# Attention with tiles 0 and 1 of the scores in the same banks, 1e-9 added by GpSimd, and a new order of all operations

## The chip, the cores and the metric

The kernel runs on one core of a Trainium2 chip. The metric is the device time of one execution in microseconds (us). The kernel before has a median of 1025.54 us over three runs (1025.2 to 1026.46).

## The reference

Three stages follow one another: a forgetting attention, a mixture layer with softplus and a second one with a gate. Cut to what is computed:

```python
# q, k, v: (4, 8, 576, 64), f: (4, 8, 576)
scores = q @ k.T / sqrt(64) + (cum[:, None] - cum[None, :])   # cum = cumsum(log(clip(f, 1e-4, 1)))
scores = where(causal, -1e9, scores); scores -= max(scores)
attn = exp(scores); attn = attn / (sum(attn) + 1e-9)
x = attn @ v                                  # -> (2304 tokens, 512)
x = softplus(x @ w_in) @ w_out                # d_ff = 2048
out = (sigmoid(x @ w_gate) * (x @ w_val)) @ w2_out   # d_ff = 1536
```

## The kernel before

All products are made in split precision: a matrix is a high part, rounded for TensorE (names with h), and a low part that is the rest (names with l), and a product is three matmuls of these parts (four for scores, with one that adds the decay rows `nb`).

The attention goes over 16 pairs p, each two heads of one batch entry. One pair is a list of operations, methods of `Attention` with the pair and a tile number:

- `load_q`, `load_k`, `load_v`, `decay_rows` are loads issued by SyncE (SP). `qh`, `kh`, `ql`, `kl`, `v_high`, `v_low` split them on GpSimd (POOL).
- `scores(i)`: row blocks of 128 queries of the two heads. Causality lets row block i of head 0 and block 8 − i of head 1 go as one step (tiles i and 8 − i); their widths are in `W9`, 128 to 512. Each is four pairs of matmuls over half the rows of the array, into two PSUM banks of the tag `s` (lines 223). The last block, tile 4, takes eight matmuls of 288 columns into the tile X (line 212).
- `minimum(t)`, VectorE (DVE), line 230: adds the causal mask, scales by −1/8 and takes the row minimum, so it reads `s`. `exp(t)`, ScalarE (ACT), line 235: exponential and row sum.
- `transposes(g)`, TensorE (PE), line 254: seven groups of up to four 128 x 128 blocks of the exponentials into a bank of the tag `t`, which has two banks. `evac_h(g)` on ScalarE (line 276) and `evac_l(g)` on VectorE (line 280) take the high and low part out.
- `rinv`: sums + 1e-9 (line 286) and reciprocal (line 287), both on VectorE. `rinv_t`: TensorE transposes the reciprocals (line 292) into a bank of the tag `t`; `rinv_b`: ScalarE copies them (line 297); `rinv_c`, `rinv_d`: through DRAM they come back spread over all rows.
- `pv(h, j)`, line 330: transposed exponentials times v for head h, into the accumulators, tile Y for head 0 and tile X for head 1. X holds tile 4 of the scores as well, at another time. X and Y have two banks each.
- `out_a(h)` on ScalarE (line 340) copies half of an accumulator, `out_b(h)` on VectorE (line 345) adds the other half to it, `out_c` on GpSimd (line 348) multiplies by the reciprocals, `out_d` stores.

The order of all instructions is written out: `WHEN` gives each operation a number, pair p adds 9 p (`PERIOD`), and `Attention.run` sorts all of them and issues them in that order; every engine keeps the order of its own part. `START` replaces numbers for pair 0 and `END` for pair 15. Each engine then works its list strictly from the front, and waits for semaphores where data or a buffer isn't ready.

Into the same order go the steps that prepare the weights of the next stage (`Weights.op`): LOAD (512 KB by SP, line 480), SCALE and HI on ScalarE (lines 488, 493), SHIFT, LOW, SIGN on VectorE (lines 502, 504, 506), LO on GpSimd (line 496). `STEPS` and `LATE_STEPS` say when which step is due; a step that can't be done (its predecessor isn't there, or `limit` is reached) is skipped. `X_STEPS` does the same for loading the next stage's tokens (cast at line 551), `PRODUCTS` and `UNITS` for its first products. Behind the attention `Moe1` and the second layer run from their own loops; they are not touched.

Of the kernel before, what the change touches and what calls it, by code (L numbers as in the profile page):

```python
# [21 lines left out]
class Attention:  # L22
# [327 lines left out]
    def out_d(self, R, p):  # L350
# [14 lines left out]
        ("kl",): -9.0904, ("decay_rows",): -8.1126, ("scores", 4): -2.7503, ("scores", 3): -2.135,
        ("minimum", 4): -2.019, ("minimum", 3): -0.0192, ("minimum", 5): 0.3552, ("scores", 1): 2.0404,
        ("exp", 3): 2.9766, ("exp", 5): 3.066, ("minimum", 1): 3.0798, ("minimum", 7): 3.2918, ("scores", 0): 4.02,
        ("minimum", 0): 4.7488, ("minimum", 8): 4.7664, ("exp", 7): 4.9241, ("scores", 2): 5.5069,
        ("minimum", 6): 5.8865, ("exp", 0): 6.2356, ("minimum", 2): 6.379, ("exp", 1): 6.6423, ("exp", 4): 6.7033,
        ("exp", 2): 7.105, ("transposes", 0): 7.5695, ("load_v",): 7.7728, ("exp", 6): 7.8053,  # L370
        ("transposes", 1): 7.9929, ("exp", 8): 8.7191, ("evac_h", 0): 9.5166, ("evac_h", 1): 9.5706,
        ("rinv",): 10.083, ("v_high",): 10.1126, ("evac_l", 0): 10.4436, ("v_low",): 10.514,
        ("evac_l", 1): 11.2219, ("transposes", 2): 12.2269, ("evac_h", 2): 12.276, ("transposes", 3): 12.3519,
        ("evac_h", 3): 12.4099, ("evac_l", 2): 13.0431, ("rinv_t",): 13.1193, ("rinv_b",): 13.2113,
        ("evac_l", 3): 13.7368, ("transposes", 5): 13.8096, ("transposes", 4): 13.9726, ("evac_h", 5): 14.8574,
        ("pv", 0, 0): 14.9016, ("evac_h", 4): 14.9515, ("evac_l", 5): 15.137, ("pv", 0, 2): 15.291,
        ("evac_l", 4): 15.6663, ("transposes", 6): 15.699, ("evac_h", 6): 16.5991, ("evac_l", 6): 16.839,
# [785 lines left out]
```

## Time and profile before

| what | value |
|---|---|
| median of the runs | 1025.54 us |
| time of the profiled execution | 1027.21 us |
| its span | 1025.3 us |
| mean granted TensorE clock | 0.996 |
| TensorE busy | 1003.1 us, 98% of the span |
| VectorE busy | 609.5 us, 59% |
| ScalarE busy | 510.4 us, 50% |
| GpSimd busy | 147.2 us, 14% |
| attention | about 0 to 217 us |

The busy shares are means over stages. In the attention VectorE, ScalarE and GpSimd are busy for most of the time too; behind it GpSimd has next to nothing to do. The rows that count are in the section before the prediction.

### The profile page before, as it was taken

The numbers are of one execution on the slowest core, as the hardware profiler recorded it, in microseconds if no ns is written. First come the engines' busy times: TensorE is split into PE (matmuls) and PEld (weight loads), VectorE is DVE, ScalarE is ACT, GpSimd is POOL, SyncE is SP. The second block draws the span as 40 slices with busy tenths as digits, with TensorE's granted clock in tenths as the row PEclk, the third lists the DMA queues.
The fourth block names the chain that finished last, engine by engine and source line by source line (L and its number), as shares of the span: only waits on it lengthen the run. The fifth ranks groups of instructions, "written<-read, shape, count | busy, mean of one in ns | idle before, by whom it ended". The sixth has DMA issues, their size and how long they took to land.

```text
span 1025.3 us, 15871 instructions
## 1 busy us (share of the span) xinstructions
PE 1003.1 (98%) x5584; PEld 880.1 (86%) x5584; DVE 609.5 (59%) x1226; ACT 510.4 (50%) x1085; POOL 147.2 (14%) x154
## 2 busy tenths in 40 slices
PE   5999999999999999999999999999999999999998
PEld 4788877887788889988888889999999999999997
DVE  5999999877955666645636654445344343443333
ACT  4889988866644455445334544333334233333332
POOL 7667776610000000000000000000000000000000
PEclk8999999999999999999999999999999999999999
DMA  5355554534535656627525776865677666676631
GB/s 149 113 144 148 158 144 132 173 118 171 208 141 187 231 187 243 251 83 263 195 102 180 257 251 230 294 226 187 222 259 255 216 213 223 211 246 214 222 139 62
DMA packets 114698, 196.07 MB, mean 191 GB/s; under 512 B 14702, under 2 KB 38398, under 8 KB 114620
## 3 DMA queue, kind: packets, MB, share of 16 engines
q1 hardware_dynamic: 112684, 189.98, 55.3%
q10 hardware_dynamic: 1936, 5.09, 1.6%
q8 instruction: 44, 0.72, 0.3%
q14 instruction: 34, 0.28, 0.1%
HBM read 149.19 MB, written 45.83 MB: 190 GB/s over the span
## 4 chain that ended last, share of the span: by engine, by line
PE 87%; DMA 4%; DVE 4%; ACT 3%; issue 1%; SPq 1%; POOL 0%; ACTq 0%; DVEq 0%; POOLq 0%
PE z L559 9%; PE z L561 9%; PE z L560 9%; PE h L559 5%; PE h L560 5%; PE h L561 5%; PE x L330 5%; PE s L223 5%; PE t L254 4%; DMA raw_wi<-in_moe_w_in_dram 3%; PE oY L559 2%; PE oY L560 2%; PE oY L561 2%; PE oX L559 2%; PE oX L560 2%; PE oX L561 2%
## 5 line engine op out<-in xcount | busy, mean ns | idle before, releaser
L559 PE MATMUL z<-three,three 128*128 128x384 f32 x456 | 152.9, 335 | 0.1
L561 PE MATMUL z<-three,three 128*128 128x384 f32 x456 | 152.8, 335 | 0.0
L560 PE MATMUL z<-three,three 128*128 128x384 f32 x456 | 152.6, 335 | 0.0
L608 DVE TENSOR_TENSOR gl<-L,gh 128x512 fp32r<-128x512 f32 (+1 forms) x80 | 51.0, 637 | 109.1 <-ACT gh L607 105.4
L596 ACT ACTIVATE L<-h 128x512 f32<-128x512 f32 (+1 forms) x80 | 44.2, 553 | 140.0 <-PE h L561 140.0
L235 ACT ACTIVATE P<-P,m 128x128 f32<-128x128 f32 (+3 forms) x144 | 83.2, 581 | 9.2 <-DVE m L230 9.2
L559 PEld LDWEIGHTS z<-three,three 128*128 128x128 f32 x456 | 85.6, 188 | 1.8 <-DVE raw L869 0.5
L560 PEld LDWEIGHTS z<-three,three 128*128 128x128 f32 x456 | 85.6, 188 | 1.4
L561 PEld LDWEIGHTS z<-three,three 128*128 128x128 f32 x456 | 85.6, 188 | 0.0
L230 DVE CUSTOM_DVE_ANT_0 P<-s,mask 128x256 f32<-128x256 f32 (+3 forms) x144 | 70.6, 516 | 12.2 <-PE s L223 7.4
L559 PE MATMUL h<-xh,wi_h 128*128 128x512 f32 (+1 forms) x200 | 73.7, 368 | 0.0
L561 PE MATMUL h<-xh,wi_h 128*128 128x512 f32 (+1 forms) x200 | 73.6, 368 | 0.0
L560 PE MATMUL h<-xl,wi_h 128*128 128x512 f32 (+1 forms) x200 | 73.6, 368 | 0.0
L280 DVE TENSOR_TENSOR PTl<-t,PTh 128x512 fp32r<-128x512 f32 (+2 forms) x112 | 66.9, 619 | 5.0 <-ACT PTh L276 4.9
L856 ACT COPY bl<-z 128x384 f32<-128x384 f32 x36 | 17.3, 479 | 101.6 <-PE z L561 101.6
L868 DVE TENSOR_TENSOR raw<-z,bh 128x384 f32<-128x384 f32 x36 | 20.1, 557 | 76.3 <-PE z L561 76.3
L861 DVE TENSOR_TENSOR raw<-z,p 128x384 f32<-128x384 f32 x18 | 10.0, 558 | 93.1 <-PE z L561 79.2
L276 ACT CAST PTh<-t 128x512 fp32r<-128x512 f32 (+2 forms) x112 | 55.9, 536 | 18.1 <-PE t L254 17.7
L254 PE MATMUL t<-ident,P 128*128 128x128 f32 x400 | 60.2, 286 | 4.6 <-DVE PTl L280 3.2
L254 PEld LDWEIGHTS t<-ident,P 128*128 128x128 f32 x400 | 44.9, 143 | 17.3 <-issue 4.7
L890 ACT CAST gh<-raw 128x384 fp32r<-128x384 f32 x72 | 33.6, 514 | 48.6 <-DVE raw L873 47.2
L330 PE MATMUL x<-PTh,V 128*128 128x256 f32 (+2 forms) x224 | 56.5, 312 | 0.5 <-POOL V L171 0.5
(293 smaller groups left out, 2565.4 us busy)
## 6 DMA issues: line engine op xcount, KB each, us to landing
three<-sd_g SPq DMA_DIRECT2D x126, 256.0 KB
three<-sd_v SPq DMA_DIRECT2D x126, 256.0 KB
two<-sd_w SPq DMA_DIRECT2D x36, 256.0 KB
raw_wi<-in_moe_w_in_dram SPq DMA_DIRECT2D x16, 512.0 KB
raw_wo<-in_moe_w_out_dram SPq DMA_DIRECT2D x16, 512.0 KB
fraw<-in_moe_w_gate_dram SPq DMA_DIRECT2D x12, 512.0 KB
fraw<-in_moe_w_out_dram SPq DMA_DIRECT2D x12, 512.0 KB
sd_g<-sh SPq DMA_DIRECT2D x24, 256.0 KB
```

Of the source, the lines that this page charges most:

```text
L223: nc.tensor.matmul(ps[h][:, 0:N], L[o], r[o, 0:N], start=j == 0, stop=j == n - 1)
L230: self.nc.vector.tensor_tensor_reduce(P, src, mask, -0.125, 3e38, op0=ALU.add, op1=ALU.min, accum_out=R["m"][:, t:t + 1])
L235: self.nc.scalar.activation(P, P, AF.Exp, bias=R["m"][:, t:t + 1], scale=-1.0, accum_out=R["sum"][:, t:t + 1])
L254: nc.tensor.transpose(ps[:, 128 * n:128 * n + 128], R["P"][:, o:o + 128], self.ident)
L276: self.nc.scalar.copy(d, s)
L280: self.nc.vector.tensor_sub(l, s, h)
L330: nc.tensor.matmul(R["acc%d" % h][:, o:o + n], v, t[:, col:col + n], start=j == 0 and w == 0, stop=j == 1 and w == 1)
L559: nc.tensor.matmul(ps, ah, bh, start=start and i == 0, stop=False, **how)
L560: nc.tensor.matmul(ps, ah, bl, start=False, stop=False, **how)
L561: nc.tensor.matmul(ps, al, bh, start=False, stop=stop and i == n - 1, **how)
L596: nc.scalar.activation(g, ph, AF.Softplus)
L608: nc.vector.tensor_sub(gl, s, gh)
```

## The change

1. `scores(1)` makes two row blocks in one step: block 1 into columns 0 to 255 and block 0 into columns 256 to 511 of the same two banks of the tag `s`. `scores(0)` is gone; a pair has three groups in `s` instead of four. Matmuls and minima stay the same in number.
2. The constant tile `eps` and the addition on VectorE go. A new operation `rinv_a` on GpSimd adds 1e-9; `rinv` is only the reciprocal.
3. `rinv_t` transposes into the first columns of the accumulator tile Y of head 0 (the products use its columns 256 to 831), so the tag `t` is used seven times a pair. `rinv_b` copies from there.
4. All numbers of `WHEN`, `START`, `END`, `STEPS`, `LATE_STEPS`, `X_STEPS`, `PRODUCTS` and `UNITS` are new. The limit on weights is 10 from the start (before: 6, and 10 from the end of the attention). `open_pools` stands 6.09 behind the end of the attention in the order (before: 0.5 ahead of it), the switch `W.alone` at 500 (before: 18.1), the loading of the softplus table at 57.6 (before: 8.3).

The order on TensorE in the steady part, pair 8, before. `s_1` and `s_0` are the groups of scores with the two banks behind (`_0`, `_1`), `t_2` to `t_5` groups of transposes, `x_1` and `x_0` the accumulators X and Y, `rt` the transposed reciprocals, `s_4` the scores of tile 4 of the next pair:

```order
L223 MATMUL s_1_1_1663<-nb_111,one 128x256
L254 MATMUL t_2_1682<-ident,P_1376 128x128 x4
...
L330 MATMUL x_1_1637<-PTl,V_1459 128x256
L223 MATMUL s_0_0_1708<-Yh_1426,Xh_1397 128x256
...
L223 MATMUL s_0_1_1709<-nb_111,one 128x256
L292 MATMUL rt_1719<-ident,r_1648 9x128
L254 MATMUL t_5_1727<-ident,P_1376 128x128 x4
L254 MATMUL t_4_1734<-ident,P_1376 128x128 x3
L223 MATMUL s_2_0_1739<-Yh_1426,Xh_1397 128x384
...
L330 MATMUL x_0_1751<-PTl,V_1651 128x320
L212 MATMUL s_4_1762<-Yh_1618,Xh_1589 128x288
```

The same place on TensorE in the changed kernel. The reciprocals now go into `x_0`:

```order
L222 MATMUL s_1_1_1641<-nb_112,one 128x256
L222 MATMUL s_1_0_1640<-Yh_1382,Xh_1424 128x256
...
L222 MATMUL s_1_1_1641<-nb_112,one 128x256
L253 MATMUL t_2_1661<-ident,P_1351 128x128 x4
...
L328 MATMUL x_1_1623<-PTl,V_1368 128x256
L222 MATMUL s_2_0_1704<-Yh_1382,Xh_1424 128x384
...
L222 MATMUL s_2_1_1705<-nb_112,one 128x384
L291 MATMUL x_0_1714<-ident,r_1636 9x128
L253 MATMUL t_5_1716<-ident,P_1351 128x128 x4
L253 MATMUL t_4_1721<-ident,P_1351 128x128 x3
L210 MATMUL s_4_1733<-Yh_1572,Xh_1616 128x288
```

The second group of scores has moved up behind the first, tile 2 comes before the reciprocals and the last transposes, and tile 4 of the next pair follows these at once, without a product of the first head between.

VectorE at the same place before. `P<-s_...` is a minimum, `PTl<-t_...` an `evac_l`, `xs<-x_...` an `out_b`, the line with `raw` a step of the weights:

```order
L286 TENSOR_TENSOR r_1648<-sum_1378,eps 128x9
L287 RECIPROCAL r_1648<-r_1648 128x9
...
L280 TENSOR_TENSOR PTl<-t_1_1613,PTh 128x512
L230 ISA P_1568,m_1569<-s_1_0_1662,mask 128x256
...
L506 SCALAR_TENSOR_TENSOR w_wi_1269<-raw_wi_969,w_wi_1269 128x512
L280 TENSOR_TENSOR PTl<-t_2_1682,PTh 128x512
L280 TENSOR_TENSOR PTl<-t_3_1690,PTh 128x2x256
L230 ISA P_1568,m_1569<-s_0_0_1708,mask 128x128
...
L345 TENSOR_TENSOR xs_1679<-x_0_1560,bs_1680 64x576
L345 TENSOR_TENSOR xs_1679<-x_1_1637,bs_1680 64x576
L230 ISA P_1568,m_1569<-s_2_1_1740,mask 128x384
```

And in the changed kernel:

```order
L279 TENSOR_TENSOR PTl<-t_1_1608,PTh 128x512
L287 RECIPROCAL r_1636<-r_1636 128x9
L229 ISA P_1542,m_1543<-s_1_0_1640,mask 128x256
...
L229 ISA P_1542,m_1543<-s_1_0_1640,mask 128x128
...
L343 TENSOR_TENSOR xs_1677<-x_0_1526,bs_1678 64x576
L279 TENSOR_TENSOR PTl<-t_2_1661,PTh 128x512
L279 TENSOR_TENSOR PTl<-t_3_1680,PTh 128x2x256
L343 TENSOR_TENSOR xs_1677<-x_1_1623,bs_1678 64x576
L229 ISA P_1542,m_1543<-s_2_0_1704,mask 128x384
```

The four minima of tiles 1, 7, 0 and 8 stand together, the first `out_b` has moved ahead of the two evacuations, and the second is the last instruction on VectorE that reads X before tile 4 of the next pair may be written there. Only the first two of the four minima wait for TensorE: a single wait covers all sixteen matmuls. In four pairs a step of the weights stands between the four minima and the second `out_b`.

In SP's queue the loads at the start have moved, too: before, the first v, q and k of pair 1, and then the first weights; now the weights' first block, the first v, the second block, and then k and q of pair 1.

The diff, cut to its core:

```diff
-        self.eps = c.tile([128, 9], F32, name="eps")
-        nc.gpsimd.memset(self.eps, 1e-9)
...
-        w = self.W9[i]
-        N = max(w, 256)
         ps = [self.ps.tile([128, 512], F32, tag="s", bufs=2, name=f"s{p}_{i}_{h}") for h in range(2)]
...
+        for x, a in ((1, 0), (0, 256)) if i == 1 else ((i, 0),):
+            w = self.W9[x]
+            N = max(w, 256)
+            q = slice(128 * x, 128 * x + 128)
+            for j, (L, r) in enumerate(((Xh[:, q], Yh), (Xl[:, q], Yh), (Xh[:, q], Yl), (self.one[:, 0:128], nb))):
+                for h in range(2):
+                    o = slice(64 * h, 64 * h + 64)
+                    nc.tensor.matmul(ps[h][:, a:a + N], L[o], r[o, 0:N], start=j == 0, stop=j == n - 1)
             for h in range(2):
...
+                R["src", (x, 8 - x)[h]] = R["P"], ps[h][:, a:a + w], self.mask[:, 512 - w:512]
...
+    def rinv_a(self, R, p):
+        R["r"] = self.sm.tile([128, 9], F32, tag="r", name=f"r{p}")
+        self.nc.gpsimd.tensor_scalar(R["r"], R["sum"], 1e-9, 1.0, op0=ALU.add, op1=ALU.mult)
+
     def rinv(self, R, p):
-        nc = self.nc
-        r = self.sm.tile([128, 9], F32, tag="r", name=f"r{p}")
-        nc.vector.tensor_add(r, R["sum"], self.eps)
-        nc.vector.reciprocal(r, r)
-        R["r"] = r
+        self.nc.vector.reciprocal(R["r"], R["r"])
 
     def rinv_t(self, R, p):
-        ps = self.ps.tile([128, 512], F32, tag="t", bufs=2, name=f"rt{p}")
-        self.nc.tensor.transpose(ps[0:9, 0:128], R["r"], self.ident)
-        R["rt"] = ps
+        R["acc0"] = self.wide.tile([128, 1024], F32, tag="Y", name=f"x{p}_0")
+        self.nc.tensor.transpose(R["acc0"][0:9, 0:128], R["r"], self.ident)
...
-        self.nc.scalar.copy(rt, R["rt"][0:9, 0:128])
+        self.nc.scalar.copy(rt, R["acc0"][0:9, 0:128])
...
-        ("load_q",): -23.5799, ("load_k",): -16.9757, ("qh",): -11.2698, ("kh",): -9.873, ("ql",): -9.3162,
+        ("load_k",): -12.6369, ("load_q",): -6.8215, ("decay_rows",): -3.1251, ("kh",): -3.0558, ("kl",): -2.6423,
...
-    W.limit = EARLY
+    W.limit = EARLY + MORE
...
-            W.limit = EARLY + MORE
...
-        others += [(end - .5, open_pools), (end + 18.1, W.alone)]
+        others += [(end + 6.0857, open_pools), (end + 500, W.alone)]
...
-        others += [(end + 8.3, lambda: nc.scalar.preload_act_table_set("softplus"))]
+        others += [(end + 57.6069, lambda: nc.scalar.preload_act_table_set("softplus"))]
```

## Rows read from the trace of the kernel before

**Rows 1.** The page's second part: TensorE's busy tenths in 40 equal slices of the span

```profile
PE   5999999999999999999999999999999999999998
```

**Rows 2.** Windows: start:end, length, busy of PE, PEld, DVE, ACT, POOL, clock, DMA share, GB/s

```profile
0.00:32.00 32.00, 19.86 (x114) 14.81 (x114) 18.71 (x48) 15.35 (x39) 20.40 (x47) 0.89 0.51 145
32.00:204.00 172.00, 168.03 (x1341) 140.91 (x1341) 162.85 (x431) 150.35 (x415) 121.16 (x104) 1.00 0.51 145
55.41:67.05 11.64, 11.64 (x96) 9.86 (x95) 11.32 (x31) 10.07 (x30) 7.92 (x8) 1.00 0.54 136
125.44:187.97 62.53, 59.50 (x475) 49.49 (x473) 59.16 (x158) 53.23 (x146) 44.98 (x39) 1.00 0.52 148
```

**Rows 3.** Timeline of TensorE: start, length, operation, tile, idle before it and its releaser

```profile
72.60 0.39 PE L223 MATMUL s<-Yh,Xh 64*128 64x256 f32 x2
72.82 0.28 PE L223 MATMUL s<-Yh,Xl 64*128 64x256 f32 x2
...
73.06 0.28 PE L223 MATMUL s<-nb,one 64*128 64x256 f32 x2
73.27 1.09 PE L254 MATMUL t<-ident,P 128*128 128x128 f32 x8
...
75.29 0.38 PE L223 MATMUL s<-Yh,Xh 64*128 64x256 f32 x2
...
75.96 0.28 PE L292 MATMUL rt<-ident,r 128*9 128x128 f32 x1
...
77.06 0.44 PE L223 MATMUL s<-Yh,Xh 64*128 64x384 f32 x2
...
77.96 0.54 PE L330 MATMUL x<-PTh,V 128*128 128x256 f32 x2
...
78.60 0.29 PE L212 MATMUL s<-Yh,Xh 128*128 128x288 f32 x1
```

**Rows 4.** Timeline of GpSimd, VectorE and ScalarE in the same pair

```profile
70.55 1.42 POOL L348 TENSOR_TENSOR xs<-xs,rb 128x576 f32<-128x576 f32 x1
71.08 0.93 DVE L286 TENSOR_TENSOR r<-sum,eps 128x9 f32<-128x9 f32 x1
...
73.37 0.42 DVE L230 CUSTOM_DVE_ANT_0 P<-s,mask 128x256 f32<-128x256 f32 x1
...
74.06 0.80 DVE L506 SCALAR_TENSOR_TENSOR w_wo<-raw_wo,w_wo 128x512 uint32<-128x512 uint32 x1
74.78 1.27 DVE L280 TENSOR_TENSOR PTl<-t,PTh 128x512 fp32r<-128x512 f32 x2
...
75.40 0.63 ACT L340 COPY bs<-x 64x576 f32<-64x576 f32 x1 [0.37 <-PE x L330]
...
76.06 0.29 DVE L230 CUSTOM_DVE_ANT_0 P<-s,mask 128x128 f32<-128x128 f32 x1
...
76.49 1.53 DVE L345 TENSOR_TENSOR xs<-x,bs 64x576 f32<-64x576 f32 x2
```

**Rows 5.** Line 286 from 40 to 118 us: least, median, largest ns

```profile
L286 DVE TENSOR_TENSOR r<-sum,eps x7: 918/940/1361, 47.9 to 117.8; 128x9 f32<-128x9 f32 x7
```

**Rows 6.** Timeline of the disturbed pairs, all engines

```profile
126.18 1.57 POOL L171 TENSOR_TENSOR Xl<-qr,Xh 128x640 fp32r<-128x640 f32 x1
...
126.56 1.74 DVE L504 SCALAR_TENSOR_TENSOR w_wo<-raw_wo,w_wo 128x512 uint32<-128x512 uint32 x1
...
128.91 0.63 PE L254 MATMUL t<-ident,P 128*128 128x128 f32 x4 [0.54 <-DVE PTl L280]
...
175.40 0.54 PE L330 MATMUL x<-PTh,V 128*128 128x256 f32 x2 [0.54 <-POOL V L171]
```

**Rows 7.** Timeline of TensorE at the start of the attention

```profile
19.81 1.76 PE L254 MATMUL t<-ident,P 128*128 128x128 f32 x7 [1.24 <-ACT P L235]
...
29.12 0.73 PE L223 MATMUL s<-Yh,Xh 64*128 64x256 f32 x2 [0.42 <-DVE m L230]
...
31.98 0.40 PE L212 MATMUL s<-Yh,Xh 128*128 128x288 f32 x1
```

More of the change, by code (lines that the diff above doesn't have):

```diff
@@ L363 @@
     WHEN = {
-        ("load_q",): -23.5799, ("load_k",): -16.9757, ("qh",): -11.2698, ("kh",): -9.873, ("ql",): -9.3162,
[L365 to L377, printed above, removed]
-        ("pv", 0, 4): 17.6509, ("pv", 0, 3): 18.0197, ("pv", 0, 1): 18.5838, ("pv", 1, 0): 18.8295,
@@ new lines @@
+        ("scores", 2): 12.7666, ("exp", 8): 12.9734, ("exp", 0): 13.0651, ("minimum", 2): 13.7044,
+        ("minimum", 6): 13.9082, ("v_high",): 14.3150, ("exp", 2): 15.1991, ("exp", 7): 15.7357, ("exp", 6): 16.2055,
+        ("transposes", 0): 16.2622, ("transposes", 1): 17.3912, ("evac_h", 0): 18.2789, ("evac_h", 1): 18.5171,
+        ("rinv_a",): 18.5480, ("evac_l", 0): 18.6507, ("transposes", 2): 19.4713, ("evac_l", 1): 19.7593,
+        ("rinv",): 19.7737, ("transposes", 3): 20.4336, ("evac_h", 2): 20.6053, ("v_low",): 21.0902,
@@ new lines @@
+        ("evac_h", 3): 21.1562, ("evac_l", 2): 21.5016, ("evac_l", 3): 21.5232, ("rinv_t",): 21.7761,
+        ("transposes", 5): 21.8611, ("transposes", 4): 21.8718, ("evac_h", 5): 22.4047, ("evac_l", 5): 22.9161,
+        ("pv", 0, 0): 23.3925, ("evac_h", 4): 23.6391, ("pv", 0, 2): 24.0387, ("transposes", 6): 24.3167,
+        ("evac_l", 4): 24.3534, ("evac_h", 6): 25.1486, ("pv", 0, 4): 25.4382, ("evac_l", 6): 25.7540,
+        ("pv", 0, 3): 26.5356, ("pv", 0, 1): 26.7739, ("pv", 1, 0): 26.9352, ("pv", 1, 2): 27.4316,
@@ new lines @@
+    END = {
+        ("load_k",): -19.2056, ("load_q",): -5.0515, ("kh",): -3.0204, ("qh",): 1.7046, ("ql",): 1.7478,
+        ("decay_rows",): 3.5852, ("kl",): 4.2281, ("scores", 4): 4.8170, ("scores", 3): 6.7992,
+        ("minimum", 4): 8.4365, ("minimum", 5): 8.9081, ("exp", 4): 9.9315, ("exp", 5): 12.1405,
+        ("minimum", 3): 12.2340, ("scores", 1): 12.5542, ("minimum", 7): 12.6493, ("minimum", 1): 12.8050,
+        ("exp", 3): 13.4789, ("minimum", 8): 13.8762, ("minimum", 0): 13.9071, ("exp", 1): 14.9786,
+        ("scores", 2): 15.0847, ("minimum", 2): 16.3043, ("exp", 2): 17.6428, ("exp", 0): 18.1401,
+        ("exp", 8): 18.7617, ("transposes", 2): 18.9284, ("load_v",): 19.0245, ("transposes", 0): 20.0591,
+        ("v_high",): 21.0760, ("minimum", 6): 21.1282, ("evac_h", 2): 23.3501, ("evac_l", 2): 24.0401,
+        ("evac_h", 0): 24.6576, ("evac_l", 0): 26.3497, ("transposes", 4): 31.1791, ("exp", 6): 31.4365,
+        ("exp", 7): 35.0552, ("evac_h", 4): 38.0734, ("rinv_a",): 46.9720, ("transposes", 1): 48.0668,
+        ("v_low",): 50.4644, ("evac_h", 1): 53.2163, ("evac_l", 4): 56.5929, ("transposes", 5): 58.2967,
+        ("rinv",): 64.1196, ("evac_l", 1): 65.0059, ("evac_h", 5): 67.2125, ("transposes", 3): 70.6715,
+        ("rinv_t",): 70.9382, ("evac_l", 5): 72.1287, ("evac_h", 3): 72.6345, ("evac_l", 3): 72.7267,
+        ("pv", 0, 0): 72.9643, ("pv", 0, 2): 75.3203, ("transposes", 6): 76.9165, ("pv", 0, 3): 86.2592,
+        ("rinv_b",): 87.0025, ("evac_h", 6): 92.4256, ("evac_l", 6): 104.1634, ("pv", 0, 4): 104.3844,
+        ("rinv_c",): 109.1615, ("pv", 0, 1): 117.5480, ("out_a", 0): 123.0169, ("rinv_d",): 126.3337,
+        ("out_b", 0): 128.7619, ("pv", 1, 0): 133.7322, ("pv", 1, 3): 134.5713, ("pv", 1, 2): 137.6671,
+        ("pv", 1, 4): 139.6979, ("pv", 1, 1): 146.8778, ("out_a", 1): 165.2565, ("out_b", 1): 181.7202,
+        ("out_c",): 187.8540, ("out_d",): 197.4597}
```

72 lines of the change are left out of this document (26 added, 46 removed), and 20 rows, old and new, of tables (END, LATE_STEPS, START, STEPS).

## The prediction, made before the changed kernel had run

> **What bounds the kernel now.** I read the busy slices first: TensorE stands at nine tenths or more in every slice but the first and the last [rows 1], so a microsecond that TensorE doesn't work or doesn't wait is a microsecond of the span, and work of another engine counts only where TensorE waits for it. Then I went by stages. The change touches the attention, which is the first fifth of the span; what comes behind it keeps its instructions and is bound by TensorE. From 32 to 204 us, all of it attention, TensorE is idle for 172.00 − 168.03 = 3.97 us in all [rows 2]. That is the most that any better order can win there; more can only come from TensorE work that gets shorter, or from the first 32 us, where TensorE works 19.86 us [rows 2].
>
> An undisturbed pair of heads takes 11.64 us, TensorE is busy for all of it, and VectorE for 11.32 of it [rows 2]. So TensorE sets the pace and VectorE follows with 0.3 us to spare. The five pairs from 125.44 to 187.97 us take 62.53 us, 4.3 more than 5 × 11.64 = 58.2, and TensorE is idle for 62.53 − 59.50 = 3.03 us of that [rows 2]. Three quarters of all idle time in the attention lies there.
>
> **Part 1: tiles 0 and 1 in one run.** A group of eight matmuls of 256 columns costs from 72.60 to 73.27, 0.67 us. The first pair of matmuls takes 0.22 (to 72.82), the next pairs 0.12 each (two of them in 0.24, to 73.06), and the last 0.21 until the following transposes start [rows 3]. A run of sixteen is one more set of four inner pairs: 0.67 + 4 × 0.12 = 1.15 us, against 2 × 0.67 = 1.34 before (the second group too is 75.29 to 75.96, 0.67 [rows 3]). It saves 0.19 us a pair, if the change of rows in the middle of the run costs what an inner pair costs; the other bound is 0.22 for that pair, 0.10 more, which leaves 0.09. I take 0.19, since the inner steps already change the weights each time. Over the 14 pairs of the steady order that is −2.7 us (bounds −1.3 and, over 16 pairs, −3.0).
>
> The price is a later start of the minima: both halves of a bank are written before the first may be read, so the first minimum waits 4 × 0.12 = 0.48 us longer than it needs. In the old order VectorE reached it as soon as the group was done (73.37 behind 73.27 [rows 3, 4]), so a later group pushes VectorE by as much, unless it finds other work; part 4 counts this.
>
> The Trainium skill, page "PSUM — Partial Sum Buffer", section "PSUM bank collisions raise a hardware error", says that two engines must not touch one bank and quadrant at once, at whatever address, and so asks for guards by bank. By it the wait for all sixteen matmuls can't be had back by a finer wait, and the same holds for the reciprocals in part 3; no run here shows a collision, and the sum is the same with or without the rule.
>
> **Part 2: the addition of 1e-9.** On VectorE it took 0.93 us at 71.08 [rows 4], for 9 numbers a row, and its seven instances from 40 to 118 us have a median of 0.94 [rows 5]. It ends at 72.01, and the GpSimd multiplication beside it (70.55, 1.42 us) at 71.97 [rows 4]: the addition waits out the GpSimd instruction. Without it VectorE has 10.4 us of work in an 11.45 us pair instead of 11.32 in 11.64. This is worth nothing by itself, as TensorE doesn't wait for VectorE in the undisturbed pair. GpSimd gets one small instruction more a pair. By the multiplication of 576 columns it lies between 0 and 1.42 us [rows 4]; nine columns of 576 would be 0.02, so I take 0.1, near the low end, and count 0 for the span: GpSimd is busy 7.92 of 11.64 us [rows 2]. What is queued behind it there waits for the pair's last exponential, too: V's low part, needed only after seven transposes, and the next loads' roundings, needed a pair later. The reciprocal on VectorE now waits for GpSimd, with the minima behind it; the sum it needs is old by then. The transposition of the reciprocals comes 2.02 + 0.90 us behind the run of sixteen [rows 3].
>
> The Trainium skill, page "SBUF — State Buffer", section "Who interferes with whom", says that a VectorE instruction with two SBUF inputs shares a read port with GpSimd's reads and that the loser blocks for the whole instruction. These rows agree: the eps addition has two such inputs and ended with the GpSimd instruction [rows 4]. By the rule the weights' LOW and SIGN steps keep this cost, whichever pair they stand in.
>
> **Part 3: reciprocals into the Y tile.** The transposition itself stays. The tag of the transposes is used seven times instead of eight, so one evacuation less must be over at that point. In exchange ScalarE's copy of the reciprocals moves behind the copy of the first head, nearly a pair later, and the multiplication on GpSimd and the output follow a pair later. Nothing on TensorE waits for these until the tail. I count 0 (bounds −0.3, one wait in the tail, and +0.5).
>
> **Part 4: the new order.** The place that can hurt is the accumulator X. In the new order TensorE goes from the run of sixteen to eight transposes with the second head's products (73.27 to 75.29, 2.02), tile 2 (77.06 to 77.96, 0.90), the reciprocals with seven transposes (75.96 to 77.06, 1.10) and straight to tile 4 of the next pair, which needs X: 4.02 us [rows 3]. In the old order there are 78.60 − 73.27 = 5.33 us [rows 3]. From the same point VectorE must do four minima (73.37 to 74.06, 0.69; 76.06 to 76.49, 0.43), the first addition from Y (half of 1.53), two subtractions (74.78 to 76.06, 1.28) and the addition from X (0.77) before X is free: 0.69 + 0.43 + 0.77 + 1.28 + 0.77 = 3.94, and about 0.1 to start behind TensorE [rows 4]. So 4.04 against 4.02: no slack. ScalarE's copy from X is no bound: 75.40 + 0.63 is 0.74 behind the products' end at 75.29, and with 0.77 on VectorE makes 1.51 against tile 2 and the transposes' 2.00 [rows 3, 4]. I count 0.08 for the ten pairs with nothing else between (the 0.02, and a semaphore's 0.06 as the middle of nothing and that 0.1), 0.8. In four pairs a step of the weights (0.80 for the one at 74.06 [rows 4]) is queued between the minima and the addition, and delays tile 4 by its whole length if VectorE arrives late, by nothing if it has run ahead; I take 0.25 a time, nearer to nothing as VectorE has a microsecond of room in a pair, which makes 1.0. Together +1.8, bounds 0 and 14 × 0.77 = 10.8 (one addition late each time).
>
> The disturbed pairs: VectorE's LOW at 126.56 took 1.74 us beside GpSimd's subtraction of 1.57 at 126.18, and the transposes at 128.91 then waited 0.54 for VectorE; at 175.40 TensorE waited 0.54 for V on GpSimd [rows 6]. The new order spreads these steps over earlier pairs, VectorE has a microsecond more room per pair, and V stands earlier in GpSimd's queue. The bounds are 0 and −3.0, the idle time; I take −2.0, two thirds, since some of the new order's steps will meet a GpSimd instruction too.
>
> The start: before, TensorE waits 0.42 for the second group's bank at 29.12, 1.24 for the first exponentials at 19.81, and is back at tile 4 of the third pair at 31.98 [rows 7]. The granted clock averages 0.89 in the first 32 us against 1.00 from there on [rows 2]: part of that work runs at the lower of its two levels, 1.2 GHz, and the change alters nothing that I can see in when. With the merge (0.19), no bank to wait for (0.42) and the transposes of the first pair some tenths earlier I get −1.5 (0.42 + 0.19, and 0.9 of the 1.24). The other way: SP's queue now has the first two weight blocks ahead of pair 1's k and q. At the 145 GB/s of the stretch [rows 2], 512 KB take 3.6 us each. TensorE needs pair 1 only at about 14 us, so I take this as hidden; the bounds of the start are −4.0 and +3.6.
>
> The tail: the same ten weight blocks are as far at the end of the attention, and the products of the next stage stand at the same place behind it: 0, bounds −1.0 and +1.5.
>
> **The sum.** −2.7 − 2.0 − 1.5 + 1.8 = −4.4 against the profiled execution's 1027.21, 1022.8. That execution lies 1.67 above the median of the runs, 1025.54, which the forecast has to meet: **1021.1 us**.
>
> **Rivals.**
> - *More comes back.* All of the disturbed pairs' idle time (3.0), a start at its better bound (4.0), merge over 16 pairs (3.0), X never late: −10.0, 1015.5. For it: VectorE's microsecond of room. Against: the 4.02 against 4.04 at X.
> - *Nothing.* The order only moves the collisions (disturbed 0), one weight block delays the start by half its 3.6 us (+1.8): −2.7 + 1.8 + 1.8 = +0.9, about 1026.4. For it: the trace has the GpSimd collisions wherever a LOW stands. Against: the start needs pair 1 late.
> - *Slower: X is late in each pair.* The addition from X just before tile 4 makes TensorE wait a whole addition, 0.77, each time. 10.8 instead of 1.8 is 9.0 more: 1030.1. It decides from 6.2 / 14 = 0.44 us a pair on. For it: no slack at all, and four weight steps in the chain. Against: VectorE's total falls under TensorE's, so it needn't enter the chain late.
> - *The merged run isn't shorter* (the middle costs 0.22 and another 0.1): the merge gives 0, 1023.8, inside the forecast's own range.
>
> **Chances.** Forecast, with the last rival, 0.50; more 0.15; nothing 0.14; X late 0.21. A change of under 0.2%, 2.05 us, can't be told from none here. Faster by more: 0.15, most of 0.50 (0.47), and a little of the third (0.05), 0.67. Within 0.2%: 0.03 of the forecast, 0.07 of the third and 0.03 of X late at the break-even, 0.13. Slower: the rest, 0.20. The forecast's own range is 1017.5 to 1024.5; the one for 8 in 10 reaches from 1014.0, below the second case, to 1028.5, short of the worst.
>
> **What would show it.** Sixteen matmuls within 1.1 to 1.2 us of each other; no addition on VectorE ahead of the reciprocal, VectorE under 10.6 us a pair; tile 4 waiting less than 0.2 us for the addition from X in most pairs. Pairs of about 11.5 us from 40 to 205 us, and tile 4 of the third pair at about 30.5 us. I am wrong if tile 4 waits over 0.4 us again and again, if TensorE's gaps wander to waits for GpSimd's one or ScalarE's evacuation, or if the third pair begins later than 32 us.

## The result, and the profile after

The changed kernel takes 1033.16 us (median of ten runs, 1030.16 to 1037.73), the kernel before 1026.43 in the same comparison (1024.51 to 1027.71): a ratio of 1.0069, 95% interval 1.0051 to 1.0088. It is 7 us slower, where 4.4 us faster was forecast. The profiled execution took 1034.51 with a span of 1032.7, 7.4 us above the span before.

The windows of the changed kernel, columns as in [rows 2], with one undisturbed pair (third row) and the worst one (fourth):

```profile
0.00:32.00 32.00, 19.64 (x118) 15.53 (x118) 17.74 (x48) 17.31 (x44) 21.23 (x47) 0.95 0.57 161
32.00:204.00 172.00, 161.97 (x1315) 137.72 (x1313) 152.45 (x416) 148.82 (x398) 124.91 (x117) 0.98 0.48 132
101.87:113.31 11.44, 11.26 (x95) 9.70 (x95) 9.68 (x29) 10.27 (x30) 6.96 (x7) 1.00 0.47 131
137.25:154.73 17.48, 13.54 (x95) 11.77 (x95) 10.87 (x33) 9.83 (x28) 10.96 (x12) 0.80 0.60 158
204.00:320.00 116.00, 111.30 (x509) 90.76 (x508) 81.70 (x144) 67.64 (x121) 9.41 (x8) 0.99 0.46 161
```

From 32 to 204 us TensorE is now idle for 10.0 us instead of 3.97 [rows 2]. The undisturbed pair did become shorter, 11.44 instead of 11.64, and VectorE has its room, 9.68 us of work. One pair takes 17.48 us, at a granted clock of 0.80.

I cut each span at tile 4 of pair 3 and of pair 15, which the timeline of TensorE shows, to see which part of the kernel a difference comes from (us; one profiled execution each, which can lie some us from the median: 5.5 below it in loads_early, 3.8 in outc14, 2.1 in x_early, 1.4 above it in the changed kernel):

| kernel | start | pairs 3 to 15 | from pair 15 on | span |
|---|---|---|---|---|
| before | 43.51 | 144.46 | 837.33 | 1025.3 |
| changed | 42.13 | 149.20 | 841.37 | 1032.7 |
| x_early | 42.39 | 144.71 | 840.00 | 1027.1 |
| outc14 | 39.99 | 146.41 | 839.80 | 1026.2 |
| loads_early | 40.61 | 142.19 | 835.10 | 1017.9 |
| xs3 | 42.02 | 144.59 | 835.29 | 1021.9 |
| unmerged | 41.53 | 150.21 | 836.26 | 1028.0 |
| before_x_late | 44.20 | 149.76 | 834.24 | 1028.2 |

The change gains 1.4 at the start, and loses 4.7 in twelve pairs and 4.0 behind them. One execution of a tail is no sharp measure: the six kernels in the old order (before, before_loads, before_x_late and the parts alone) lie between 834.2 and 837.7 in the third column, the six in the new order with its tail not yet mended between 839.8 and 841.4, the five with it mended between 835.1 and 836.2. The groups don't overlap, so that a loss of some 4 us is shown; but a single difference of up to 3.5 us in this column need not come from the edit.

**The pair of 17.48 us.** Timeline of VectorE, SP and TensorE in the changed kernel (start, length, operation, idle before it and what ended it):

```profile
148.24 0.43 DVE L550 CAST xh<-xr 128x512 fp32r<-128x512 f32 x1 [5.58 <-DMA xr<-xT]
148.58 0.68 DVE L279 TENSOR_TENSOR PTl<-t,PTh 128x512 fp32r<-128x512 f32 x1
```

```profile
144.13 0.60 SPq L355 DMA_DIRECT2D xT<-xs  x1
144.82 0.56 SPq L541 DMA_DIRECT2D xr<-xT  x1
```

```profile
149.32 0.90 PE L253 MATMUL t<-ident,P 128*128 128x128 f32 x3 [3.94 <-DVE PTl L279]
```

VectorE stands 5.58 us before the cast of the next stage's tokens. Their load is issued only at 144.82, behind the stores of an earlier pair, which wait for their multiplication (on GpSimd from 141.52 to 142.94); an evacuation stands behind the cast, and TensorE waits 3.94 for it. It has been idle since 145.4, and its granted clock falls, here by windows of 1 us:

```profile
146.00:147.00 1.00, 0.00 (x0) 0.00 (x0) 0.00 (x0) 0.00 (x0) 0.00 (x0) 1.00 0.89 242
148.00:149.00 1.00, 0.00 (x0) 0.00 (x0) 0.76 (x2) 0.00 (x0) 0.25 (x1) 0.50 0.67 164
...
153.00:154.00 1.00, 1.00 (x8) 0.68 (x5) 0.85 (x4) 0.88 (x6) 1.00 (x3) 0.50 0.88 281
```

The clock is still at 1.2 GHz (0.50) nearly five microseconds after the work went on at 149.32, and TensorE's own work in this pair takes 13.54 us instead of 11.26. Wait and slower work, 3.94 and 2.28, less the wait of 0.18 that an undisturbed pair has, are the 6.0 us above 11.44. In the new `X_STEPS` load and cast stand at −35.28 and −35.01; before, at −42.74 and −28.10 (numbers of the order, of which a pair has 9).

**Behind pair 15.** GpSimd, VectorE and TensorE at the tail of the changed kernel:

```profile
213.76 1.41 POOL L346 TENSOR_TENSOR xs<-xs,rb 128x576 f32<-128x576 f32 x1 [5.66 <-DMA rb<-rd]
215.26 0.20 POOL L284 TENSOR_SCALAR r<-sum 128x9 f32<-128x9 f32 x1
215.54 1.54 POOL L169 TENSOR_TENSOR V<-vr,V 128x640 fp32r<-128x640 f32 x1
```

```profile
215.49 0.21 DVE L287 RECIPROCAL r<-r 128x9 f32<-128x9 f32 x1 [3.49 <-POOL r L284]
```

```profile
216.31 0.66 PE L253 MATMUL t<-ident,P 128*128 128x128 f32 x4 [1.76 <-DVE PTl L279]
```

The multiplication of pair 14 (`out_c`) waits for the reciprocals, which come back through DRAM; the last pair's addition of 1e-9 and V stand behind it on GpSimd, the reciprocal behind the addition, an evacuation behind that. This is not all of the loss: cut once more where the last product with v ends, the 4.0 us are 1.2 ahead of it (30.8 against 29.6) and 2.8 behind it (810.6 against 807.8). Behind it TensorE waits 1.62 at 269.05 for ScalarE, which had stood for loads issued by SP from 260.18 on, and its clock is at 0.50 from 271 to 274.

### The profile page after: what moved, and what is told of

Its sections match the earlier page's. It is cut to its first block, busy times and chain, and to the rows that moved or that the text cites. A ratio compares the mean times of both kernels' runs of the same rounds, so it can differ in the third digit from the quotient of the medians.

```text
span 1032.7 us, 15898 instructions
## 1 busy us (share of the span) xinstructions
PE 1001.8 (97%) x5584; PEld 881.9 (85%) x5584; DVE 597.6 (58%) x1208; ACT 513.5 (50%) x1085; POOL 155.5 (15%) x171
## 4 chain that ended last, share of the span: by engine, by line
PE 82%; DVE 7%; DMA 5%; issue 2%; ACT 2%; SPq 1%; POOL 1%; DVEq 0%; ACTq 0%
PE z L558 9%; PE z L560 8%; PE z L559 8%; PE h L558 6%; PE h L560 6%; PE h L559 6%; PE s L222 3%; PE x L328 2%; PE oY L560 2%; PE oY L559 2%; PE oY L558 2%; PE t L253 2%; PE o L559 2%; PE oX L559 2%; PE oX L560 2%
## 5 line engine op out<-in xcount | busy, mean ns | idle before, releaser
L595 ACT ACTIVATE L<-h 128x512 f32<-128x512 f32 (+1 forms) x80 | 44.3, 553 | 144.5 <-PE h L560 144.4
L234 ACT ACTIVATE P<-P,m 128x576 f32<-128x576 f32 (+3 forms) x144 | 83.4, 582 | 12.6 <-DVE m L229 12.2
L229 DVE CUSTOM_DVE_ANT_0 P<-s,mask 128x256 f32<-128x256 f32 (+2 forms) x144 | 68.6, 515 | 17.8 <-PE s L222 13.1
L253 PE MATMUL t<-ident,P 128*128 128x128 f32 x400 | 64.7, 289 | 10.1 <-DVE PTl L279 8.6
L889 ACT CAST gh<-raw 128x384 fp32r<-128x384 f32 x72 | 33.5, 514 | 48.6 <-DVE raw L872 47.2
L328 PE MATMUL x<-PTh,V 128*128 128x320 f32 (+2 forms) x224 | 56.9, 308 | 0.4 <-ACT rt_sb L295 0.3
L328 PE MATMUL x<-PTl,V 128*128 128x320 f32 (+2 forms) x224 | 54.6, 294 | 0.0
L708 DVE TENSOR_TENSOR l<-fw,sh 128x512 fp32r<-128x512 f32 x60 | 40.7, 687 | 13.9 <-ACT sh L707 11.4
L606 ACT CAST gh<-L 128x512 fp32r<-128x512 f32 (+1 forms) x80 | 46.3, 578 | 2.5
```

The lines of the kernel that those rows point to most:

```text
L229: self.nc.vector.tensor_tensor_reduce(P, src, mask, -0.125, 3e38, op0=ALU.add, op1=ALU.min, accum_out=R["m"][:, t:t + 1])
L234: self.nc.scalar.activation(P, P, AF.Exp, bias=R["m"][:, t:t + 1], scale=-1.0, accum_out=R["sum"][:, t:t + 1])
L253: nc.tensor.transpose(ps[:, 128 * n:128 * n + 128], R["P"][:, o:o + 128], self.ident)
L328: nc.tensor.matmul(R["acc%d" % h][:, o:o + n], v, t[:, col:col + n], start=j == 0 and w == 0, stop=j == 1 and w == 1)
L595: nc.scalar.activation(g, ph, AF.Softplus)
L606: nc.scalar.copy(gh, s)
```

## The experiments

**The load of the tokens.** One number of the changed kernel:

```diff
-X_STEPS = [-65.3948, -49.4998, -35.2788, -35.0096, ...
+X_STEPS = [-65.3948, -49.4998, -45.0, -35.0096, ...
```

> The changed kernel with one number other: the load of the second quarter of the next stage's tokens stands at -45.0 in X_STEPS instead of -35.28, so 10 places of the order ahead of its cast on VectorE instead of 0.27. Theory (a load waited for): VectorE no longer waits 5.58 us for that load, TensorE not 3.94 us behind it, the granted clock doesn't fall, and the pair that took 17.48 us takes 11.4 to 11.8: 6.0 us less than the changed kernel, about 1027 (ratio to before 1.000 to 1.002). Rival (the new order as a whole is late, the load was only the last of several waits): VectorE meets the next late operand there, the pair stays above 14 us and the time above 1030.

Measured: 1031.02 (ratio 1.0034, 1.0021 to 1.0047). The pair takes 12.34 instead of 17.48 (11.4 to 11.8 expected), and the wait for the load is gone, as the theory had it; but the ratio falls by 0.0035, 3.6 us, where 6.0 were expected. What the late load costs differs from execution to execution. r15_dve (below) has the same order here, and in its profile VectorE, TensorE and the whole pair are:

```profile
146.34 0.43 DVE L551 CAST xh<-xr 128x512 fp32r<-128x512 f32 x1 [4.39 <-DMA xr<-xT]
```

```profile
147.42 0.66 PE L253 MATMUL t<-ident,P 128*128 128x128 f32 x4 [2.74 <-DVE PTl L279]
```

```profile
136.53:151.33 14.80, 11.72 (x94) 9.77 (x95) 9.94 (x30) 10.17 (x29) 9.54 (x10) 1.00 0.61 168
```

TensorE waits 2.74 there, the granted clock stays at 1.00, and the pair is 3.4 us above 11.44, not 6.0. The counter-test puts load and cast together in the kernel before:

```diff
-X_STEPS = [-60.0345, -42.888, -42.7421, -28.1038, ...
+X_STEPS = [-60.0345, -42.888, -33.95, -33.7, ...
```

> The kernel before, but the load of the second quarter of the next stage's tokens and its cast on VectorE are put next to each other in the order (-33.95 and -33.7), behind the store of the pair before, as in the changed kernel. Theory (a load waited for): VectorE stands 3 to 5 us before the cast, TensorE 2 to 4, the granted clock falls for some us, and the time is 3 to 6 us longer, 1030 to 1033 (ratio 1.003 to 1.006). Rival (the load was late in the changed kernel for another reason, its crowded queue): within 1 us of before.

Measured: 1031.94 (1.0048, 1.0032 to 1.0065). In its trace, VectorE, then TensorE:

```profile
162.33 0.43 DVE L551 CAST xh<-xr 128x512 fp32r<-128x512 f32 x1 [3.58 <-DMA xr<-xT]
```

```profile
163.15 0.92 PE L223 MATMUL s<-Yh,Xh 64*128 64x256 f32 x2 [2.38 <-DVE m L230]
```

That pair takes 18.75 us there, 12.87 before, with the granted clock at 0.50 from 163 to 169 us. All of it is as expected: the mechanism is shown from both sides.

**The tail.** First the addition alone, then both edits:

```diff
+        e = self.nc.vector if p == self.NP - 1 else self.nc.gpsimd
+        e.tensor_scalar(R["r"], R["sum"], 1e-9, 1.0, op0=ALU.add, op1=ALU.mult)
```

> The changed kernel, but for the last pair alone the addition of 1e-9 is made by VectorE, not GpSimd. Theory (a queue): the addition no longer stands behind the multiplication of the pair before, which waits 5.66 us for the reciprocals to come back through DRAM; the reciprocal on VectorE loses its wait of 3.49 us, TensorE its 1.76 at the last transposes. 1.5 to 2 us less than the changed kernel, about 1031.3 (ratio 1.0050). Rival: the last pair waits for something else as long (the exponentials, the weights), and the time stays at 1033 (ratio 1.0069).

> Both edits together. Theory: the gains add, 7.5 to 8 us less than the changed kernel, 1025 to 1026 (ratio 0.998 to 1.000). Rival: a later wait for data takes the place of one of them and the time stays at 1028 or more.

Measured: 1032.54 (1.0057, 1.0039 to 1.0076) and 1030.17 (1.0033, 1.0018 to 1.0048). The second is its rival's; the first interval holds theory and rival alike, and the trace decides for the rival. TensorE in r15_dve at the tail:

```profile
216.66 0.53 PE L329 MATMUL x<-PTh,V 128*128 128x256 f32 x2 [2.96 <-POOL V L169]
```

V stands in the same queue, behind the same multiplication, and is now the last to come. So the multiplication itself was moved (on top of x_early):

```diff
+                self.NP - 2: {("out_c",): 60.0, ("out_d",): 61.0}}
```

> The changed kernel with the earlier token load of x_early, and with the multiplication by the reciprocals and the store of pair 14 (out_c, out_d) put 17 places later in the order, behind the last pair's addition of 1e-9 and the low part of its v. Theory (GpSimd's queue at the tail): these two stood behind a multiplication that waits 5 to 6 us for its operand from DRAM; without it TensorE loses the waits for the reciprocal's successors (1.84 us in x_early) and for V (2.96 in r15_dve), so 2 us less than x_early, 1029 or below (ratio 1.000 to 1.002). Rival: the tail waits for something else again (the weights, the copy of the reciprocals), and the ratio stays at 1.0034.

Measured: 1031.74 (1.0031, 1.0016 to 1.0046): the rival again. Both waits are gone, and the wait turned up at the next queue. In the profiles, from pair 15 to the end of the last product with v outc14 takes 28.8 us, x_early 33.5; behind it outc14 takes 811.0, x_early 806.6: 4.7 won and 4.4 lost. ScalarE, SP and TensorE in outc14:

```profile
230.86 0.66 ACT L488 ACTIVATE w_wi<-raw_wi 128x512 f32<-128x512 f32 x1 [7.19 <-DMA raw_wi<-in_moe_w_in_dram]
```

```profile
225.12 0.60 SPq L355 DMA_DIRECT2D xT<-xs  x1
225.83 1.44 SPq L480 DMA_DIRECT2D raw_wi<-in_moe_w_in_dram  x1
```

```profile
233.92 0.50 PE L559 MATMUL o<-gh,wi_h 128*128 128x512 f32 x1 [2.34 <-ACT gh L607]
```

The weight load is issued behind the last pair's stores, which wait for the same way through DRAM, and the softplus stands behind it on ScalarE. So SP's queue was put right as well:

```diff
-                self.NP - 2: {("out_c",): 60.0, ("out_d",): 61.0}}
+                self.NP - 2: {("out_c",): 60.0, ("out_d",): 128.0}}
...
+              (166, 2), (166.1, 2), (167, 3), (167.1, 3), (168, 4), (168.1, 4), (169, 0), (169.1, 0)]
```

> outc14 with SP's queue at the tail put right as well: pair 14's stores behind the weight loads of that time, and six weight steps and two loads added at the end of LATE_STEPS, ahead of the last pair's stores. In outc14 ScalarE stood 7.19 us for a weight block whose load was issued only behind the last pair's stores, and TensorE then 2.34. Theory (loads held behind stores that wait for the reciprocals' way through DRAM): ScalarE's wait falls below 3 us, TensorE's goes, 2.5 us less than outc14 in a run like its profile, ratio 0.999 to 1.001. Rival (the DMA rate, not the issue, sets when the blocks are there): the wait stays above 5 us, ratio 1.003.

Measured: 1025.25 (0.9986, 0.9972 to 1.0001), as expected; ScalarE's longest wait for a block is 2.4 us, and from pair 15 on it takes 835.1 us, 4.7 less than outc14. The same for the kernel before, with the steps at 48.5 to 49.9:

> The kernel before with six weight steps and the three loads behind them added to LATE_STEPS ahead of the last pair's stores, as in loads_early. Theory (the same hold-up is there before, ScalarE waits 1.4 and 2.3 us for blocks issued behind the last stores, but TensorE has work all the while): no change or up to 1 us less, ratio 0.999 to 1.001. Rival (it is a cost that the kernel before pays too): 2 us or more less, ratio below 0.998.

Measured: 1028.6 (1.0021, 1.0011 to 1.0030): slower, outside both expectations. Why is not known: its profiled execution, the fastest of its twelve, is like the one before in all three parts (42.9, 144.5, 837.7). The old tail has no such cost to win back: behind the last product with v TensorE never waits over 0.23 us there in the profile before.

**The parts alone, in the old order.** merge_alone is the changed `scores` in the old order without `("scores", 0)`; eps_alone has `rinv_a` at 8.8 and `rinv` at 11.25; merge_eps both.

> The kernel before with the first part of the change alone: tiles 1 and 0 in one run of sixteen matmuls in the same banks, the old order otherwise. Theory of the prediction: a pair takes 11.45 instead of 11.64, 14 times, 2.5 us less than before, 1023.9 (ratio 0.9976). Rival: tile 2 now needs the banks that the minima of tiles 0 and 8 free late in VectorE's old order, TensorE waits for it 0.2 us or more in each pair, and the ratio is 1.000 or above.

> The kernel before with the second part of the change alone: GpSimd adds 1e-9 ahead of its subtraction for the next pair's k, and the reciprocal on VectorE comes behind the second evacuation; the rest in the old order. Theory of the prediction: VectorE gets 1 us of room a pair but TensorE doesn't wait for it in the undisturbed pairs, so these stay at 11.64; in the five disturbed pairs some of the 3 us of waiting goes: 0 to 3 us less than before, ratio 0.997 to 1.000. Rival: GpSimd's queue, held by the addition until the last exponential, makes the next pair's scores late; above 1.002.

> Both parts, the merged run and the addition on GpSimd, in the old order. Theory (the merged run makes VectorE start its minima half a microsecond later, and VectorE had only 0.3 us of room): the microsecond that the addition gives back pays for that, the waits of 0.32 us in each pair of merge_alone go, and a pair takes 11.45 to 11.55 instead of 11.95: 1023 to 1026 (ratio 0.997 to 1.000). Rival (tile 2 waits for the banks of tiles 0 and 8, whatever VectorE has to do): pairs stay at 11.9 and the ratio at 1.005.

Measured: 1033.28 (1.0059, 1.0045 to 1.0072), 1028.8 (1.0019, 1.0008 to 1.0029) and 1040.39 (1.0129, 1.0116 to 1.0142). An undisturbed pair takes 11.9 to 12.0, 11.64 and 12.96. merge_alone came out as its rival in the time, but not in the place: TensorE's wait of 0.32 is ahead of the last seven transposes, for VectorE's evacuation, and not at tile 2. eps_alone lies between its two expectations: the undisturbed pairs stay, and three of the disturbed ones grow (13.3, 13.4 and 13.1 us, 12.8, 12.9 and 12.7 before). VectorE, GpSimd and TensorE in merge_eps:

```profile
78.37 0.42 DVE L231 CUSTOM_DVE_ANT_0 P<-s,mask 128x256 f32<-128x256 f32 x1 [1.36 <-PE s L224]
...
79.07 1.68 DVE L506 SCALAR_TENSOR_TENSOR w_wo<-raw_wo,w_wo 128x512 uint32<-128x512 uint32 x1
```

```profile
74.77 0.20 POOL L286 TENSOR_SCALAR r<-sum 128x9 f32<-128x9 f32 x1 [1.03 <-ACT P L236]
...
78.64 1.56 POOL L171 TENSOR_TENSOR V<-vr,V 128x640 fp32r<-128x640 f32 x1
```

```profile
81.41 0.28 PE L293 MATMUL rt<-ident,r 128*9 128x128 f32 x1 [1.04 <-DVE PTl L281]
```

VectorE has room, and spends it waiting 1.36 us for all sixteen matmuls; then the weight step that the old order has there meets GpSimd's work on V and takes 1.68 instead of 0.69 in merge_alone, and TensorE waits 1.04. The step stands at the same place of the pair in both, 7.58 us behind tile 4; what moved is V, from 5.80 to 7.15, since GpSimd's addition, ahead of it in the queue, waits 1.03 us for the last exponential. In the pairs where a SHIFT stands there, it is the same (1.46 at 92.04, 0.43 in merge_alone). The theory, that room for VectorE pays for the later minima, fell: the room lies before the scores and the lateness behind them. The Trainium skill, page "SBUF — State Buffer", section "Who interferes with whom", says that a VectorE instruction with two SBUF inputs contends with a GpSimd instruction that reads SBUF; the step at 79.07 has two, and ended 0.55 us behind GpSimd's, so that this trace agrees.

**The steps, and parts undone in the new order.** steps_moved changes six numbers of STEPS and LATE_STEPS in loads_early; eps_back restores the constant and `tensor_add` in outc14; xs3 and unmerged are edits of loads_early, unmerged_xs3 is both:

```diff
-R["xs"] = self.xp.tile([128, self.S], F32, tag="xs", name=f"xs{p}")
+R["xs"] = self.xp.tile([128, self.S], F32, tag="xs", name=f"xs{p}", bufs=3)
```

```diff
-        for x, a in ((1, 0), (0, 256)) if i == 1 else ((i, 0),):
+        for x, a in ((i, 0),):
...
+        ("scores", 0): 12.53, ("minimum", 0): 12.60, ("minimum", 8): 12.61, ("scores", 2): 12.95,
```

> loads_early with six weight steps of VectorE moved from between the merged scores' minima and the scores of tile 4 (or right behind) to just before these minima, where VectorE waits 0.4 to 0.5 us for the sixteen matmuls. Theory (steps in the chain to X cost their length, 0.4 to 1.6 us each): 2 to 4 us less than loads_early, the pairs of 12.0 to 12.7 us fall to 11.5, and it is faster than before, ratio 0.995 to 0.998. Rival (they push the minima instead, which are in the same chain): within 1 us of loads_early.

Measured: 1025.26 (0.9996, 0.9985 to 1.0008). No gain; the pair of 12.71 became one of 11.43, and the pair before it one of 13.34. The rival held.

> outc14 with the second part of the change undone: VectorE adds 1e-9 again, right before the reciprocal. Theory (in the new order VectorE's way from the merged scores to the addition from X has no slack): the addition takes 0.9 us beside a GpSimd instruction, half of it hidden by VectorE's wait for the sixteen matmuls; tile 4 is 0.4 to 0.5 us later in each pair, 11.9 instead of 11.44, 5 to 6 us more than outc14, ratio 1.008 to 1.009. Rival (VectorE has room there): pairs stay at 11.44 to 11.5 and the ratio at 1.003.

Measured: 1030.68 (1.0046, 1.0030 to 1.0063), 1.5 us above outc14 with intervals that overlap, and pairs of 11.45 to 11.48: the rival. VectorE in such a pair:

```profile
108.31 0.20 DVE L289 TENSOR_TENSOR r<-sum,eps 128x9 f32<-128x9 f32 x1
...
109.81 0.42 DVE L231 CUSTOM_DVE_ANT_0 P<-s,mask 128x256 f32<-128x256 f32 x1 [1.06 <-PE s L224]
```

The wait for the sixteen matmuls hides the addition. It takes 0.20 us here, not 0.9, for the GpSimd instruction beside it ends at 108.48; over the sixteen pairs it takes 0.15 to 1.47.

> loads_early with three buffers instead of two for the output tile xs. Theory (the reciprocals and with them the stores come a pair later in the new order, so that VectorE's first addition finds its buffer still being stored and tile 4 is late): VectorE's waits for the stores (0.8 us once in loads_early, 3.8 us in four pairs in outc14) go; 0.5 to 3 us less than loads_early and less spread between runs, ratio 0.996 to 0.998. Rival (VectorE only arrives earlier at the next wait): within 0.5 us of loads_early, ratio 0.9985.

Measured: 1023.59 (0.9974, 0.9960 to 0.9988), the fastest of all, by 2.7 us on before. VectorE's waits from 110 to 183 us in xs3 (total us, times, longest), where outc14 had 3.8 us for the stores:

```profile
DVE r L287 <- POOL r L284: 4.3, 4, 2.9
DVE P L229 <- PE s L222: 1.4, 3, 0.6
DVE P L229 <- PE t L253: 1.4, 3, 0.7
```

and one of them in outc14:

```profile
145.75 0.75 DVE L343 TENSOR_TENSOR xs<-x,bs 64x576 f32<-64x576 f32 x1 [1.24 <-DMA xT<-xs]
```

The stores' waits are gone; its ratio's interval overlaps that of loads_early, so that the gain of 1 us itself is not sure. What is left is the first row, VectorE's wait for GpSimd's addition of 1e-9. The longest, and TensorE behind it:

```profile
170.51 0.22 DVE L287 RECIPROCAL r<-r 128x9 f32<-128x9 f32 x1 [2.93 <-POOL r L284]
```

```profile
171.71 0.62 PE L222 MATMUL s<-Yh,Xh 64*128 64x384 f32 x2 [1.30 <-DVE m L229]
```

This pair takes 13.55 us: GpSimd had stood 3.71 us for a DMA at 163.81, and the addition is the seventh instruction in its queue from there.

> loads_early with the first part of the change undone: tiles 1 and 0 as two groups of eight, the second between the second head's products and the transposition of the reciprocals, tile 2 behind the transposes, as in the old order. Theory (the merged run saves TensorE 0.19 us and lets it wait 0.18 for X at tile 4): with two groups TensorE works 0.19 longer, reaches tile 4 0.67 us later and doesn't wait; undisturbed pairs take 11.45, as before the undoing, and a weight step or a late store in VectorE's chain is hidden up to 0.6 us: 2 to 4 us less than loads_early, ratio 0.994 to 0.997. Rival (the merge is a gain): pairs of 11.6 to 11.65, 2 us more than loads_early, ratio 1.000 or above.

> Both edits. Theory: as unmerged, with the stores' waits hidden already, ratio 0.994 to 0.997. Rival: the waits for the stores add to those for X, and it is 1 us or more below unmerged.

Measured: 1029.05 (1.0020, 1.0008 to 1.0032) and 1028.02 (1.0012, 0.9999 to 1.0025). In unmerged_xs3 undisturbed pairs take 11.43, as the theory had it, and TensorE, busy for all of it, doesn't wait for X (unmerged, where stores are waited for, has none under 11.5). One such pair:

```profile
115.82:127.25 11.43, 11.43 (x96) 9.78 (x94) 10.71 (x30) 10.34 (x29) 7.91 (x8) 1.00 0.48 131
```

Yet the whole is 3.5 us slower than loads_early, and unmerged_xs3 4 us slower than xs3, so both theories failed. The disturbed pairs are longer (in unmerged_xs3 13.0 and 13.2, where loads_early has 11.46 and 12.17). In the first of them VectorE's weight step takes 2.01 us, 0.68 in loads_early:

```profile
46.46 2.01 DVE L504 SCALAR_TENSOR_TENSOR w_wi<-raw_wi,w_wi 128x512 uint32<-128x512 uint32 x1
```

So the merged run is worth nothing in an undisturbed pair of the new order. That what the weight steps meet decides which way round is faster fits these pairs, but was not isolated.

## Why the prediction was wrong, point by point

**Merge, −2.7: the matmuls right in size, the gain in the pair by luck.** TensorE and VectorE in the undisturbed pair, answering to [rows 3] and [rows 4]:

```profile
108.07 0.39 PE L222 MATMUL s<-Yh,Xh 64*128 64x256 f32 x2
...
109.21 0.66 PE L253 MATMUL t<-ident,P 128*128 128x128 f32 x4
...
113.31 0.37 PE L210 MATMUL s<-Yh,Xh 128*128 128x288 f32 x1 [0.18 <-DVE xs L343]
```

```profile
109.32 0.42 DVE L229 CUSTOM_DVE_ANT_0 P<-s,mask 128x256 f32<-128x256 f32 x1 [1.30 <-PE s L222]
...
112.40 0.76 DVE L343 TENSOR_TENSOR xs<-x,bs 64x576 f32<-64x576 f32 x1
```

The sixteen take 1.14 (1.15 forecast), the pair 11.44 (11.53 with the waits forecast), so 12 × 0.20 = 2.4 us were won over twelve pairs. But TensorE works 0.38 less and waits 0.18 for X, and unmerged_xs3 has the same 11.43 without the merge: the merge's 0.19 was spent at X, and the 0.20 comes from TensorE's work in the new order alone, a term that the prediction did not have.

**X, +1.8: right in mechanism, somewhat low.** Tile 4 waits 0.18, and 0.33 or 0.34 in some later pairs, 2.5 in twelve pairs; the rival that put a whole addition of 0.77 there did not come about, although the time came out beyond its price of 1030.1. VectorE waits 1.30 us before the chain, so it entered it on time.

**Disturbed pairs, −2.0: wrong in sign.** Without the load's wait (x_early) the twelve pairs are 7.4 us above 12 × 11.44 (4.9 in loads_early, 7.3 in xs3, 9.1 in outc14); before they were 4.8 above 12 × 11.64. The new order moves the collisions of weight steps with GpSimd and does not lower their number: four LOW and SIGN steps over 1.0 us in x_early, two before (so "wherever a LOW stands" was too strong: three of the five LOW steps before took 0.69 to 0.80). The one of 1.57 us at 53.73 makes its pair 12.72 us long (in steps_moved, without it, this pair takes 11.43); the one of 1.17 at 95.42 costs nothing, its pair takes 11.43. The last five pairs, 11.9 to 12.9 long, hold none, and have 4.9 of the 7.4 us; VectorE waits there 1.9 us for stores and 1.3 for GpSimd's addition, and how much of the 4.9 these make was not isolated. This is the first half of the rival "Nothing".

**The load of the tokens: not in the sum at all.** I took the new order's numbers for X and the weights apart, and did not follow the DMA that is waited for in VectorE's queue: load to cast shrank from 14.6 places to 0.27. It cost 6.0 us in the profiled execution, 3.4 in that of r15_dve; taking it away brought the ratio from 1.0069 to 1.0034, 3.6 us. None of the four rivals has it.

**Part 3 and the tail, 0: the step that failed most.** "Nothing on TensorE waits for these until the tail", and the tail was put at 0, bounds −1.0 and +1.5. It measured +4.0 in the profiles (841.37 against 837.33): in-order queues on GpSimd and SP passed the reciprocals' delay on to V, to the reciprocal and to the weight loads. Mending all three took the ratio from 1.0034 to 0.9986, 4.9 us; the intervals don't overlap. The later stores also reach back into the pairs: VectorE finds the output tile still being stored. Those waits are 0.85 us at most in x_early, 1.24 in outc14, none in xs3. They don't explain the wider spread of the changed kernel: xs3 without them still spreads over 7.0 us, the changed kernel over 7.6.

**Part 2, 0 for the span: right in the steady pairs** (eps_back), not in every late pair, where VectorE stood up to 2.93 us for the addition (xs3), and wrong at the tail, where the addition on GpSimd stood behind a multiplication: I named what is queued behind it, not what it is queued behind.

**Start, −1.5: right in number, in part by luck** (42.13 against 43.51, 1.4). Profiles of like kernels lie 2 us apart there, with the mean clock of the first 32 us between 0.84 and 1.00; at the same mean clock of 0.95 the old order (before_loads) has 42.9 and the changed one 42.1, a gain of 0.8. Tile 4 of the third pair came at 31.50, not at 30.5.

With the load, the tail and the output tile put right the change is a gain of 0.26% (xs3), the sign forecast and somewhat over half of its size. The kernel before was not run with a third buffer; its VectorE doesn't wait for a store from 40 to 190 us.

## What to carry to other kernels

When an order is written anew, list for every load the distance to its first use, and for every wait through DRAM what stands behind it in each in-order queue; the steady pair's sum tells neither. A step that gets off the critical engine needs to be asked twice: what waits behind it, and what it waits behind. Mending one wait at such a tail only shows the next in the chain until every queue that the late value passes is mended.
